# Product of probabilities and values with the values as weights, in a fused attention and two-layer kernel

## The chip, the cores and the metric

The kernel runs on one core of one Trainium2 chip. The metric is device time in microseconds (us), from the first to the last instruction and what lies around them; the median of several runs counts. All engines run their own instructions in program order and wait for each other by semaphores: TensorE (PE, its weight loads written PEld), VectorE (DVE), ScalarE (ACT), GpSimd (POOL), and SyncE (SP), which issues the DMAs.

## The reference

Eight batches of eight heads; 576 tokens, 64 features per head, 32 packed queries `p` per head. Two attentions come one after the other, the second reading the first one's result as keys and values, then two wide layers with an activation each.

```python
def sm_attn(qq, kk, vv):
    s = scale * np.matmul(qq, kk.transpose(0, 1, 3, 2))
    s = s - np.max(s, axis=-1, keepdims=True)
    a = np.exp(s)
    a = a / (np.sum(a, axis=-1, keepdims=True) + 1e-09)
    return np.matmul(a, vv)
p_packed = sm_attn(p, k, v)
out = sm_attn(q, p_packed, p_packed)
```

The result, as 4608 rows of 512, goes through `w_in` (512x2048), a leaky ReLU and `w_out` (2048x512), and then through a second pair of the same sizes with the activation h / (1 + exp(-1.702 h)).

## The kernel before, in words

The first part, up to about 310 us, makes both attentions and the first wide product; the rest (L694, L728, L847) is the other three wide products, which the change doesn't touch.

Per batch the first part has these steps, each a generator whose `yield`s cut it into pieces. `s1` makes the scores of the packed queries (L243), their maximum, and e = exp(scores) on ScalarE (L269). The four head pairs stand on the partitions, 32 packed queries each, so a tile of 128 partitions holds four heads; `par` is the even or odd head of each pair, so e is 128 x 2 x 576. Its last piece adds the sums and takes the reciprocal r (L273, L274). `packed` transposes e on PE in pieces of 128 keys (L284) and a rest of 64 (L286), copies the result to `et` (L289 on ScalarE, L291 on VectorE), and multiplies with the values v (L301): `et` is the stationary operand (32 packed queries of one head), v the moving one (64 features), and the result has queries on the partitions. L307 multiplies by r, L310 transposes to features on the partitions, and L313 copies that to `ppk`. From `ppk` come the second attention's scores (`s2`) and, folded with w1, the tiles `m` (`prod_m`) by which the wide product L369 (`l1`) works; L378 is its activation.

The order of all engines' work is written out. For batches 0 to 2 it is the list of words START: `score0` is the next piece of `s1(0)`, `pack0` of `packed(0)`, `l5` and `r5` a wide product and its activation, `w12` a piece of the conversion of w1 from float64 words (L155, L156, L159, L162, L163), `warm2` two products that only keep PE busy (L389). From then on there is one wide product per step n (six matmuls, about 0.8 us), and `side(n)` issues the pieces due behind it. Batch b+1, b from 2 to 6, has its pieces at s = 32 b plus

```python
first, second = range(-5, 1), (1, 2, 2, 4, 5, 6, 7)
third, fourth, fifth = (9, 10, 11, 12, 13, 14, 16, 17), (9, 10, 12, 13, 16, 20, 22, 23), (15, 23, 24, 24, 25)
for piece, when in ((s1(b + 1), first), (packed(b + 1), second), (s2(b + 1, 0), third),
```

so the sums stand at s and the transposes behind the product of s + 1. A piece called when a generator has ended does nothing. `aux` gives one of five PSUM banks in turn.

Of the kernel before, what the change touches and what calls it, by code (L numbers as in the profile page):

```python
# [9 lines left out]
F32 = mybir.dt.float32  # L10
# [4 lines left out]
ALU = mybir.AluOpType  # L15
# [3 lines left out]
B, H, S, D, J = 8, 8, 576, 64, 32  # L19
DM, FF = H * D, 2048  # L20
NT = B * S
P = 128
# [56 lines left out]
def packed_attention_moe_moe_kernel(tc, qT, kT, vm, vt, pT, w_in1, w_out1, w_in2, w_out2, out):  # L79
# [4 lines left out]
    nc = tc.nc  # L84
# [26 lines left out]
    with ExitStack() as ctx:  # L111
# [87 lines left out]
        px, pa = pools["px"], pools["pa"]  # L199
# [3 lines left out]
        ident = px.tile([P, P], F32, name="ident")  # L203
# [5 lines left out]
        tk, tq, tv, tp, e1, ppk, a2, mm = {}, {}, {}, {}, {}, {}, {}, {}  # L209

        def aux(name):
            return ps.tile([P, 512], F32, tag="aux", name=name, bufs=5)
# [21 lines left out]
        def after(load, b):  # L234
            if b < B:
                load(b)

        def both(tiles, lhsT, rhs, n):

            for i in range(4):  # L240
                for par in range(2):
                    r = slice(64 * par, 64 * par + 64)
                    nc.tensor.matmul(tiles[par][32 * i:32 * i + 32, :n], lhsT=lhsT(r, i, par), rhs=rhs(r, i),  # L243
                                     start=True, stop=True)

        def s1(b):
            k, p = tk.pop(b), tp.pop(b)
            t = [[None, None], [None, None]]
            for hf in range(2):
                for par in range(2):  # L250
                    t[par][hf] = aux(f"s1_{b}_{par}_{hf}")
                both([t[0][hf], t[1][hf]], lambda r, i, par: p[r, 2 * i + par, :],
                     lambda r, i: k[r, i // 2, i % 2, hf * TH:hf * TH + TH], TH)
            if b:
                after(load_k, b + 1)
                after(load_p, b + 1)
            yield
            mx, sm = (px.tile([P, 2, 2], F32, tag=w, name=f"{w}_{b}") for w in ("mx", "sm"))
            nb, r = (px.tile([P, 2], F32, tag=w, name=f"{w}_{b}", bufs=2) for w in ("nb", "r"))
            e = px.tile([P, 2, S], F32, tag="e", name=f"e_{b}")  # L260
            e1[b] = e, r
            for par in range(2):
                for hf in range(2):
                    nc.vector.reduce_max(mx[:, par, hf:hf + 1], t[par][hf][:, :TH], axis=AX.X)
                nc.vector.tensor_scalar(nb[:, par:par + 1], mx[:, par, 0:1], mx[:, par, 1:2], -SCALE, op0=ALU.max, op1=ALU.mult)
                yield
            for par in range(2):
                for hf in range(2):
                    nc.scalar.activation(e[:, par, hf * TH:hf * TH + TH], t[par][hf][:, :TH], AF.Exp, bias=nb[:, par:par + 1],  # L269
                                         scale=SCALE, accum_out=sm[:, par, hf:hf + 1])  # L270
                yield
            for par in range(2):
                nc.vector.tensor_scalar(r[:, par:par + 1], sm[:, par, 0:1], sm[:, par, 1:2], 1e-9, op0=ALU.add, op1=ALU.add)  # L273
            nc.vector.reciprocal(r, r)  # L274

        def packed(b):

            e, r = e1.pop(b)
            et = px.tile([P, 2, 5, P], F32, tag="et", name=f"et_{b}")
            t = [aux(f"t1_{b}_{par}") for par in range(2)]  # L280
            rest = aux(f"tr_{b}")
            for par in range(2):
                for k in range(4):
                    nc.tensor.transpose(t[par][:, P * k:P * k + P], e[:, par, P * k:P * k + P], ident)  # L284
            for par in range(2):
                nc.tensor.transpose(rest[:64, P * par:P * par + P], e[:, par, 512:576], ident)  # L286
            yield
            for par in range(2):
                nc.scalar.copy(et[:, par, 0:4, :], t[par].rearrange("p (k n) -> p k n", k=4))  # L289
            yield  # L290
            nc.vector.tensor_copy(et[:64, :, 4, :], rest[:64, :2 * P].rearrange("p (a n) -> p a n", a=2))  # L291
            yield
            v = tv.pop(b)
            o = px.tile([P, 2, D], F32, tag="o", name=f"o_{b}")
            t = aux(f"pp_{b}")
            for par in range(2):
                for k in range(5):
                    n = P if k < 4 else 64
                    for i in range(4):
                        c0 = D * (2 * (i % 2) + par)  # L300
                        nc.tensor.matmul(t[32 * i:32 * i + 32, D * par:D * par + D], lhsT=et[:n, par, k, 32 * i:32 * i + 32],  # L301
                                         rhs=v[:n, i // 2, k, c0:c0 + D], start=(k == 0), stop=(k == 4))
            if b:
                after(load_v, b + 1)
            yield
            for par in range(2):
                nc.vector.tensor_scalar(o[:, par, :], t[:, D * par:D * par + D], r[:, par:par + 1], None, op0=ALU.mult)  # L307
            yield
            t = aux(f"t2_{b}")
            nc.tensor.transpose(t[:, :P], o.rearrange("p a d -> p (a d)"), ident)  # L310
            yield
            ppk[b] = pw.tile([P, 4, J], F32, tag="ppk", name=f"ppk_{b}", bufs=2)
            nc.scalar.copy(ppk[b], t[:, :P].rearrange("p (i j) -> p i j", i=4))  # L313
# [98 lines left out]
        for b in range(2, B - 1):  # L412
            s = 32 * b
# [3 lines that stand above are left out]
                                (s2(b + 1, 1), fourth), (prod_m(b + 1, 0), fifth)):  # L417
                pieces(piece, [s + k for k in when])
# [146 lines left out]
        for b in range(3):  # L565
            going |= {f"score{b}": s1(b), f"pack{b}": packed(b)}
            going |= {f"attn{b}{hf}": s2(b, hf) for hf in range(2)}
            going |= {f"m{b}{c}": prod_m(b, c) for c in range(4 if b < 2 else 1)}
# [3 lines left out]
        for word in START:  # L572
# [4 lines left out]
            elif word[0] == "l":  # L577
                n = int(word[1:])
                banked[n] = l1(*order[n])
                side(n)  # L580
            elif word[0] == "r":
                n = int(word[1:])
# [97 lines left out]
        for k, (blk, p, f) in enumerate(steps):  # L680
# [10 lines left out]
            n = BLOCKS["b"][blk][1]  # L691
            for c in range(2):
                for m, (ws, xs) in enumerate(((0, 0), (0, 1), (1, 0))):
                    nc.tensor.matmul(acc[BANK[p]][:, c, :n], lhsT=w[:, ws, c], rhs=x[xs],  # L694
                                     start=(p in OPENS and f + m == 0), stop=(f == NJ - 1 and m == 2), skip_group_check=True)
# [65 lines left out]
        for m in range(1, 3 * NJ):  # L761
            n = first[m // NJ, m % NJ]
# [74 lines left out]
        for k, (blk, p, f) in enumerate(last_steps, LATER):  # L837
# [5 lines left out]
            n = BLOCKS["d"][blk][1]  # L843
# [63 lines left out]
```

## Time and profile before

| what | us |
|---|---|
| median of 3 runs | 1380.24 |
| lowest | 1379.56 |
| highest | 1765.2 |
| profiled execution | 1380.77 |
| its span, first to last instruction | 1378.6 |
| PE busy | 1354.9 (98%) |
| DVE busy | 1047.1 (76%) |
| ACT busy | 768.7 (56%) |
| mean granted clock of PE | 0.995 |

The profile is of one execution. A matmul in fp32 stands as two loads and two passes. Records of PE overlap: their lengths hold the way through the array, and what a pass costs is the distance from one start to the next. The form `128*32` beside a name is the part of the array that is used, rows by columns.

### The profile page before, as it was taken

The numbers are of one execution on the slowest core, as the hardware profiler recorded it, in microseconds if no ns is written. First come the engines' busy times: TensorE is split into PE (matmuls) and PEld (weight loads), VectorE is DVE, ScalarE is ACT, GpSimd is POOL, SyncE is SP. The second block draws the span as 40 slices with busy tenths as digits, with TensorE's granted clock in tenths as the row PEclk, the third lists the DMA queues.
The fourth block names the chain that finished last, engine by engine and source line by source line (L and its number), as shares of the span: only waits on it lengthen the run. The fifth ranks groups of instructions, "written<-read, shape, count | busy, mean of one in ns | idle before, by whom it ended". The sixth has DMA issues, their size and how long they took to land.

```text
span 1378.6 us, 23200 instructions
## 1 busy us (share of the span) xinstructions
PE 1354.9 (98%) x8746; PEld 1245.2 (90%) x8746; DVE 1047.1 (76%) x1548; ACT 768.7 (56%) x1363; POOL 98.5 (7%) x71
## 2 busy tenths in 40 slices
PE   6899999999999999999999999999999999999998
PEld 4688888889999989889999999999999899999998
DVE  6867777766989898989776657565559987878786
ACT  4756666676645545445566666666556443434342
POOL 2301111100000212100001000000000000000000
PEclk8999999999999999999999999999999999999999
DMA  9879999789646566564477777868886727263432
GB/s 335 303 238 311 315 318 319 255 289 328 210 165 205 174 204 225 165 235 144 137 259 237 257 244 251 266 212 261 267 289 208 222 65 215 72 189 98 139 102 46
DMA packets 251503, 302.46 MB, mean 219 GB/s; under 512 B 56832, under 2 KB 214528, under 8 KB 251392
## 3 DMA queue, kind: packets, MB, share of 16 engines
q1 hardware_dynamic: 248992, 300.70, 66.4%
q8 instruction: 68, 1.11, 0.3%
q10 hardware_dynamic: 2400, 0.30, 0.1%
q14 instruction: 43, 0.35, 0.1%
HBM read 184.55 MB, written 116.39 MB: 218 GB/s over the span
## 4 chain that ended last, share of the span: by engine, by line
PE 88%; DMA 4%; DVE 3%; ACT 3%; SPq 1%; issue 1%; POOL 0%; DVEq 0%; POOLq 0%; ACTq 0%
PE y L694 25%; PE h L728 24%; PE sum L847 18%; PE h L369 10%; PE first L847 7%; PE m L243 1%; DMA raw<-in_w_in_dram 1%; PE s L243 1%; DMA g_scratch<-g 1%; ACT g L378 1%; PE pp L301 1%; SPq L173 1%; ACT m L354 1%; DMA k<-in_kT_dram 1%; DMA q<-in_qT_dram 1%
## 5 line engine op out<-in xcount | busy, mean ns | idle before, releaser
L728 PE MATMUL h<-ya,wj 128*128 128x384 f32 x2016 | 349.9, 334 | 0.1
L728 PEld LDWEIGHTS h<-ya,wj 128*128 128x128 f32 x2016 | 349.4, 188 | 0.5 <-DVE g L750 0.4
L369 PEld LDWEIGHTS h<-a,m 128*128 128x128 f32 x1536 | 209.0, 190 | 33.8 <-issue 12.5
L500 ACT CAST da<-dr 128x960 fp32r<-128x960 f32 (+1 forms) x139 | 134.1, 966 | 179.1 <-PE sum L847 111.8
L369 PE MATMUL h<-a,m 128*128 128x288 f32 x1536 | 223.1, 301 | 8.8 <-ACT g L378 4.4
L694 PE MATMUL y<-ba,wo 128*128 128x480 f32 (+1 forms) x1080 | 225.9, 370 | 0.0
L694 PEld LDWEIGHTS y<-ba,wo 128*128 128x128 f32 x1080 | 205.4, 195 | 19.7 <-DVE ba L140 0.8
L500 ACT CAST ba<-br 128x960 fp32r<-128x960 f32 (+1 forms) x140 | 135.3, 966 | 150.5 <-PE y L694 130.7
L140 DVE TENSOR_TENSOR da<-dr,da 128x960 fp32r<-128x960 f32 (+1 forms) x139 | 154.1, 1111 | 44.1 <-ACT da L500 39.6
L140 DVE TENSOR_TENSOR ba<-br,ba 128x960 fp32r<-128x960 f32 (+1 forms) x140 | 164.9, 1180 | 19.5 <-ACT ba L500 17.6
L847 PE MATMUL sum<-da,wo 128*128 128x480 f32 (+1 forms) x840 | 176.0, 369 | 0.0
L847 PEld LDWEIGHTS sum<-da,wo 128*128 128x128 f32 x840 | 159.8, 193 | 14.8 <-DVE da L140 0.9
L378 ACT ACTIVATE g<-h 128x288 f32<-128x288 f32 x256 | 103.2, 422 | 79.9 <-PE h L369 62.7
L694 PE MATMUL y<-ba,wo_early 128*128 128x480 f32 (+1 forms) x600 | 125.7, 370 | 0.3 <-DVE ba L140 0.3
L694 PEld LDWEIGHTS y<-ba,wo_early 128*128 128x128 f32 x600 | 114.1, 195 | 11.0 <-DVE ba L140 0.7
L163 POOL TENSOR_TENSOR b_wo<-raw_wo 128x512 int32<-128x512 int32 x32 | 42.8, 1336 | 561.1 <-DVE raw_wo L162 308.3
L140 DVE TENSOR_TENSOR wj<-stage,wj 128x512 fp32r<-128x512 f32 x96 | 59.4, 619 | 26.3 <-ACT wj L667 25.8
L847 PE MATMUL sum<-da,wo_early 128*128 128x480 f32 (+1 forms) x360 | 75.4, 369 | 0.0
L847 PEld LDWEIGHTS sum<-da,wo_early 128*128 128x128 f32 x360 | 68.6, 193 | 6.0
L750 DVE TENSOR_TENSOR g<-v,h 128x384 f32<-128x384 f32 x48 | 26.5, 551 | 52.0 <-PE h L728 51.9
L357 DVE TENSOR_TENSOR m<-m,m 128x512 fp32r<-128x512 f32 x64 | 42.4, 685 | 29.6 <-ACT m L354 28.2
L734 ACT ACTIVATE g<-g 128x384 f32<-128x384 f32 x96 | 50.3, 524 | 18.7 <-ACT wj L667 6.2
(131 smaller groups left out, 1484.5 us busy)
## 6 DMA issues: line engine op xcount, KB each, us to landing
g_scratch<-g SPq DMA_DIRECT2D x64, 576.0 KB, 5.8
g_scratch<-g SPq DMA_DIRECT2D x96, 384.0 KB, 3.3
br<-g_scratch SPq DMA_DIRECT2D x64, 480.0 KB, 6.6
dr<-g_scratch SPq DMA_DIRECT2D x64, 480.0 KB, 4.7
stage<-wi_scratch SPq DMA_DIRECT2D x72, 256.0 KB, 4.0
wo_scratch<-b_wo SPq DMA_DIRECT2D x32, 448.0 KB, 4.8
k<-in_kT_dram SPq DMA_DIRECT2D x16, 576.0 KB, 7.5
q<-in_qT_dram SPq DMA_DIRECT2D x16, 576.0 KB, 6.4
```

Of the source, the lines that this page charges most:

```text
L140: at(step + 1, lambda: nc.vector.tensor_sub(*rest))
L163: nc.gpsimd.tensor_tensor(to.bitcast(I32), v.bitcast(I32), d, op=ALU.add)
L243: nc.tensor.matmul(tiles[par][32 * i:32 * i + 32, :n], lhsT=lhsT(r, i, par), rhs=rhs(r, i), start=True, stop=True)
L357: nc.vector.tensor_sub(m[:, 1, par, :], t[par], m[:, 0, par, :].bitcast(F32))
L369: nc.tensor.matmul(t[:, :TH], lhsT=m[:, ws, par, o:o + P], rhs=a[:, xs, par, :], start=(k == 0), stop=(k == 5))
L378: nc.scalar.activation(g1t[g][:, f % 2, hf * TH:hf * TH + TH], t[:, :TH], AF.Prelu, alpha=0.01)
L500: nc.scalar.copy(hi, src)
L694: nc.tensor.matmul(acc[BANK[p]][:, c, :n], lhsT=w[:, ws, c], rhs=x[xs], start=(p in OPENS and f + m == 0), stop=(f == NJ - 1 and m == 2), ...
L728: nc.tensor.matmul(to, lhsT=w[:, ws, COMBO[p], P * kk:P * kk + P], rhs=x[:, xs, kk, :], start=(p in UNIT_OPENS and kk + s == 0), stop=(kk ...
L734: nc.scalar.activation(to, to if src is None else src, AF.Gelu_apprx_sigmoid)
L750: nc.vector.tensor_add(g[1][:, HB:], v, d)
L847: nc.tensor.matmul(column_of(acc4[BANK[p]], c)[:, :n], lhsT=w[:, ws, c], rhs=x[xs], start=(p in OPENS and f + m == 0), stop=(f == NJ - 1 a ...
```

## The change

Two things are changed in `s1` and `packed`. The last piece of `s1` now takes the reciprocal of each sum by itself and multiplies e by it on VectorE, 576 elements on 128 partitions, once for each `par`; so the probabilities are divided by their sum ahead of the transposes. In `packed` the product has its operands swapped: 64 columns of v are the stationary operand and 32 packed queries of `et` the moving one, with 64 features on the partitions for each `par` and the heads along the free dimension. The loop over heads i is outermost, then keys k, then `par`. The result needs neither L307 nor L310, so two pieces of `packed` go, and the copy to `ppk` is its fifth piece instead of its seventh.

```diff
-            e1[b] = e, r
+            e1[b] = e
...
-            nc.vector.reciprocal(r, r)
+                nc.vector.reciprocal(r[:, par:par + 1], r[:, par:par + 1])
+                nc.vector.tensor_scalar(e[:, par], e[:, par], r[:, par:par + 1], None, op0=ALU.mult)
...
-            o = px.tile([P, 2, D], F32, tag="o", name=f"o_{b}")
             t = aux(f"pp_{b}")
-            for par in range(2):
+            for i in range(4):
                 for k in range(5):
                     n = P if k < 4 else 64
-                    for i in range(4):
+                    for par in range(2):
                         c0 = D * (2 * (i % 2) + par)
-                        nc.tensor.matmul(t[32 * i:32 * i + 32, D * par:D * par + D], lhsT=et[:n, par, k, 32 * i:32 * i + 32],
-                                         rhs=v[:n, i // 2, k, c0:c0 + D], start=(k == 0), stop=(k == 4))
+                        nc.tensor.matmul(t[D * par:D * par + D, 32 * i:32 * i + 32], lhsT=v[:n, i // 2, k, c0:c0 + D],
+                                         rhs=et[:n, par, k, 32 * i:32 * i + 32], start=(k == 0), stop=(k == 4))
             if b:
                 after(load_v, b + 1)
-            yield
-            for par in range(2):
-                nc.vector.tensor_scalar(o[:, par, :], t[:, D * par:D * par + D], r[:, par:par + 1], None, op0=ALU.mult)
-            yield
-            t = aux(f"t2_{b}")
-            nc.tensor.transpose(t[:, :P], o.rearrange("p a d -> p (a d)"), ident)
             yield
```

## Rows read from the trace of the kernel before

**Rows 1.** The page: busy times of PE, and the chain by line.

```profile
PE 1354.9 (98%) x8746; PEld 1245.2 (90%) x8746; DVE 1047.1 (76%) x1548; ACT 768.7 (56%) x1363; POOL 98.5 (7%) x71
...
PE y L694 25%; PE h L728 24%; PE sum L847 18%; PE h L369 10%; PE first L847 7%; PE m L243 1%; DMA raw<-in_w_in_dram 1%; PE s L243 1%; DMA g_scratch<-g 1%; ACT g L378 1%; PE pp L301 1%; SPq L173 1%; ACT m L354 1%; DMA k<-in_kT_dram 1%; DMA q<-in_qT_dram 1%
```

**Rows 2.** Waits of PE, 110 to 310 us: us in total, times, longest.

```profile
PE h L369 <- ACT g L378: 1.3, 3, 0.6
```

**Rows 3.** Waits of PE, 0 to 110 us.

```profile
PE t L310 <- DVE r L273: 1.6, 1, 1.6
...
PE t L310 <- DVE o L307: 0.8, 1, 0.8
```

**Rows 4.** Stretches of 10 us: engines' busy time, clock, DMA share, GB/s.

```profile
20.00:30.00 10.00, 8.89 (x112) 5.44 (x102) 8.41 (x17) 5.13 (x10) 3.49 (x3) 0.66 0.96 370
30.00:40.00 10.00, 6.99 (x57) 5.83 (x57) 9.72 (x21) 6.38 (x15) 1.26 (x1) 0.69 0.96 350
```

**Rows 5.** L301 alone, batch 2: length, passes, loads, clock, DMA, by stretch.

```profile
79.83:80.41 0.58, 0.58 (x32) 0.49 (x32) 1.00 0.29 80
80.41:80.66 0.25, 0.25 (x15) 0.15 (x8) 1.00 1.00 387
...
81.24:81.38 0.14, 0.14 (x15) 0.14 (x8) 1.00 1.26 428
```

**Rows 6.** L301 in its first section: ns shortest, median, longest.

```profile
L301 PEld LDWEIGHTS pp<-v,et x32: 106/110/111, 79.8 to 80.2; 128*32 128x32 f32 x32
L301 PE MATMUL pp<-v,et x32: 219/219/244, 79.8 to 80.3; 128*32 128x64 f32 x32
```

**Rows 7.** L389, 10.5 to 13.6 us: the same columns.

```profile
L389 PEld LDWEIGHTS keep<-ident x24: 186/192/192, 10.6 to 13.1; 128*128 128x128 f32 x24
L389 PE MATMUL keep<-ident x24: 274/275/377, 10.6 to 13.2; 128*128 128x128 f32 x24
```

**Rows 8.** Instructions on tile e: the same columns.

```profile
L284 PEld LDWEIGHTS t<-ident,e x64: 137/141/143, 13.8 to 262.7; 128*128 128x128 f32 x64
...
L286 PEld LDWEIGHTS tr<-ident,e x16: 110/111/113, 15.4 to 262.9; 128*64 128x64 f32 x16
```

**Rows 9.** Groups, 0 to 400 us: busy us, mean ns, idle before.

```profile
L329 DVE TENSOR_TENSOR wf<-wf,s2m 128x576 f32<-128x576 f32 x16 | 12.1, 758 | 0.6
...
L159 DVE TENSOR_SCALAR raw_wo<-raw_wo 128x512 uint32<-128x512 uint32 x16 | 6.8, 427 | 18.3 <-ACT raw_wo L156 14.7 <-DMA g_scratch<-g 3.2 <-DMA raw_wo<-in_w_out_dram 0.4
```

**Rows 10.** Timeline of batch 4: start, us, instruction, idle before.

```profile
153.91 0.21 DVE L273 TENSOR_SCALAR r<-sm 128x1 f32<-128x1 f32 x1
...
154.50 1.04 PE L284 MATMUL t<-ident,e 128*128 128x128 f32 x8
154.70 0.23 ACT L269 ACTIVATION_READ_ACCUMULATOR e<-s,nb 128x1 f32 x1
...
154.97 0.21 DVE L273 TENSOR_SCALAR r<-sm 128x1 f32<-128x1 f32 x1 [0.85 <-ACT e L269]
155.22 0.17 DVE L274 RECIPROCAL r<-r 128x2 f32<-128x2 f32 x1
```

**Rows 11.** Timeline of batch 3.

```profile
117.83 0.33 DVE L273 TENSOR_SCALAR r<-sm 128x1 f32<-128x1 f32 x2
```

**Rows 12.** Timeline of batch 2 at L310.

```profile
82.83 0.30 PE L310 MATMUL t<-ident,o 128*128 128x128 f32 x1
...
82.89 6.62 PE L369 MATMUL h<-a,m 128*128 128x288 f32 x48
```

**Rows 13.** Timeline around the last conversion of w1.

```profile
59.96 0.96 DVE L159 TENSOR_SCALAR raw<-raw 128x512 uint32<-128x512 uint32 x1
...
61.79 1.29 POOL L163 TENSOR_TENSOR w<-raw,w 128x512 int32<-128x512 int32 x1 [1.16 <-ACT m L354]
...
63.45 1.95 PE L243 MATMUL m<-w,ppk 64*32 64x512 f32 x32
```

**Rows 14.** Timeline of batch 0 behind L313.

```profile
23.46 1.21 PE L243 MATMUL s<-q,ppk 64*32 64x288 f32 x16 [0.35 <-ACT ppk L313]
```

More of the change, by code (lines that the diff above doesn't have):

```diff
@@ L273, in s1 @@
                 nc.vector.tensor_scalar(r[:, par:par + 1], sm[:, par, 0:1], sm[:, par, 1:2], 1e-9, op0=ALU.add, op1=ALU.add)
-            nc.vector.reciprocal(r, r)
+                nc.vector.reciprocal(r[:, par:par + 1], r[:, par:par + 1])
+                nc.vector.tensor_scalar(e[:, par], e[:, par], r[:, par:par + 1], None, op0=ALU.mult)
         def packed(b):
-            e, r = e1.pop(b)
+            e = e1.pop(b)
             et = px.tile([P, 2, 5, P], F32, tag="et", name=f"et_{b}")
```

## The prediction, written before the result

> **What bounds the kernel now.** I read the page's busy times and chain first [rows 1]. TensorE (PE) is busy for 98% of the span, the chain runs through its products line after line, and of the lines of the change only L301 is among the shown ones, with 1%. So the change has no large share to win, and what counts is where PE works without a gap and where it waits. The waits of PE by stretch answer that: from 110 to 310 us, where batches 3 to 7 are made, PE waits for others for 1.3 us in all [rows 2]; before 110 us it does wait, and two of those waits belong to the lines that go [rows 3]. So from about 60 us on every nanosecond that the change puts on PE is paid in full, while before that the start is a chain of loads, ScalarE and VectorE work (VectorE, DVE, is busy 8.4 and 9.7 of the 10 us from 20 and from 30 [rows 4]), into which PE fits. The eight batches split so: 0 and 1 in the start, 2 at its end, 3 to 7 under a saturated PE.
>
> **Products with values as weights.** Before, one batch's products are 40 fp32 matmuls, 80 loads and 80 passes in the trace, in four strips of the array 32 columns wide. The view by stretches shows one batch in four sections, long for the four full tiles of keys, short for the last 64 [rows 5]: 0.58 + 0.25 + 0.58 + 0.14 = 1.55 us. A long section is 8 rounds on each strip, a short one 2. So 6 rounds are 0.58 - 0.25 = 0.33 us, 0.055 us each. The first passes of a section last 244 ns where the median is 219 [rows 6]: 25 ns is the load of 32 columns, seen only once per section; the next loads hide under passes of 64 moving columns. What is left of a short section, 0.25 - 0.025 - 0.055 = 0.17 us, is the end of its passes and the change of tile shape (0.06 in the last, where the next work has the same shape).
>
> After, there are again 80 loads and 80 passes, but in two strips of 64 columns, so 16 rounds become 32 for the full tiles of keys and 4 become 8 for the rest; and the loop over heads outside makes eight sections instead of four. The pass has 32 moving columns, half of 55 ns, some 28. Its load is now the long one. For loads the trace has two ends: 32 columns 25 ns, and 128 columns 377 - 275 = 102 ns [rows 7]; the lengths of the load records agree (110 and 192 ns, 82 more for 96 columns) [rows 6, 7]. On that line 64 columns take 25 + 32 x 82/96 = 52 ns, which a pass of 28 cannot hide, so a round is about 55 ns. A section's remainder falls by half a pass to 0.14. Long: 0.052 + 7 x 0.055 + 0.14 = 0.58; short: 0.052 + 0.055 + 0.14 = 0.25; four of each, less 0.11 at the end, 3.2 us. That is 1.6 us more per batch. Against it speaks the only load of 64 columns in the trace, that of the transposes, whose record (111 ns) is no longer than one of 32 columns [rows 6, 8]; by it the load is 30 ns, a round 29, and the batch 2.2 us, 0.6 more. I take the first, because transposes load faster at 128 columns too (141 against 192 ns [rows 7, 8]) and so are another kind of load. The other end is a load and a pass that take turns, 80 ns a round: 4.0 us, 2.4 more. A gain is excluded: twice the rounds of half the length stream as long as before, and four more changes of shape come on top. Six batches (2 to 7) under a saturated PE: 6 x 1.6 = 9.8 us with the figure unrounded (1.64), between 3.8 and 14.6.
>
> The rule that bears on this price is in the Trainium skill, TensorE: Matmul & The Clock Gate, section "LDWEIGHTS (loading the stationary operand)": a load takes its columns divided by 1.2 GHz, whatever the rows. By it 64 columns are an estimated 53 ns and six batches cost 9.9 us; by the transposes' row they cost 3.8. The rows at 32 and 128 columns agree with the rule, the row at 64 does not, and no product of the kernel before loads 64.
>
> **Probabilities divided by their sum.** Before, the transposes of e wait for the exponentials alone. After, each half of e (the even or the odd heads) waits for sum, reciprocal and a 128x576 multiplication on DVE. For its price: a one-source DVE instruction of 512 fp32 words takes 427 ns, a two-source one of 576 takes 758 [rows 9]. 427 x 576/512, with some 150 ns fixed, is about 0.45 us; the upper end is 0.76. I take 0.45, as the new instruction has one source, in SBUF. The Trainium skill, VectorE: DVE Perf Modes, "Mode 2×_2P", gives such an instruction two elements per cycle for fp32 too; its rule and the 427 ns row go together, and by the 758 ns row the five waits below would cost 6.3 us in place of 4.5.
>
> Where it lies: batch 4's stretch (it repeats for 5, 6 and 7 at 190, 226 and 262 us) shows the transposes starting at 154.50, the first sum at 153.91, the second at 154.97, held by the last exponential's sum, which ends at 154.93 [rows 10]. New: second sum 154.97, + 0.21 + 0.03 + 0.17 (reciprocal) + 0.03 + 0.45 = 155.86, and 0.1 until PE sees it. The second half's transposes begin at about 155.95 instead of 154.94 (four at 0.109 after 154.50). PE has nothing else in its order, so 1.0 us is lost, four times. The first half, ready at 154.80, hides in it. In batch 3 both sums come at 117.83 [rows 11]; two chains back to back end at 119.5, the second half starts near 119.6 instead of 119.1: 0.5 us. Together 4.5 us. Queued behind on PE are the next products with w1, and through them ScalarE's activations; all just move with PE. DVE itself pays 0.9 us for two multiplications and 0.2 for one more reciprocal, less 0.4 for the two scalings that go, per batch; in these stretches it has gaps of 0.4 to 0.9 us around the sums [rows 10], so this costs nothing more.
>
> **What goes.** The scaling L307, off PE's path from batch 2 on. The transpose L310: the next product follows it after 0.06 us [rows 12]; six times is 0.3 us won. The copy L313 comes two steps earlier, which no one waits for from batch 3 on. The next values' load stays behind the products in SP's queue, 1.6 us later and tens of us ahead of its use.
>
> **The start.** Batch 1: PE waits 1.61 us for L310, from 58.14 to 59.75 [rows 3]. That goes, but its products end 1.6 us later, and they stand just ahead: nothing is won. Batch 2: the multiplications stand on DVE ahead of the last conversion of w1 (L159 at 59.96, with the GpSimd step of 61.79), and GpSimd holds them as it holds L159, which takes 0.96 us there instead of 0.43 [rows 9, 13]. That conversion lands some 1.2 us later; the product of w1 that needs it starts at 63.45, 0.4 us after its present end. I put 0.85 us. Batch 0: transposes wait until about 18 us instead of 15, partly unseen, as the copies of et stand behind work on w1 in ScalarE's order anyway. Products start 0.5 later and last longer, some of it at the lower clock (0.66 granted on the mean from 20 to 30 us, between 1.2 and 2.4 GHz [rows 4]); in return the copy L313 follows them at once, without the 0.75 us wait for L310 [rows 3]. From 23.46, the next step [rows 14], I expect 0 to 1.5 us later, and take 0.65. Together 1.5, between -1 and +3.
>
> **Sum.** 9.8 + 4.5 - 0.3 + 1.5 = 15.5 us. The profiled execution's 1380.77 us (span 1378.6 and 2.2 around it) becomes 1396.3; it stands 0.5 above the median of 1380.24, so I forecast 1395.7 us.
>
> **Rivals.**
> Narrow price for wide loads: each product batch is 0.6 dearer, not 1.6. For it the transposes' load, against it the line from 32 to 128 columns. 3.8 + 4.5 - 0.3 + 1.5 = 9.5: 1389.7 us.
> Load and pass in turn: a round of 80 ns, as two strips offer fewer places to load ahead. Against it: on four strips loads run ahead of passes now. 14.6 + 4.5 - 0.3 + 1.5 = 20.3: 1400.5 us.
> Not slower: the start decides. The chain through L307 and L310 is gone, and its PE waits of 1.6, 0.75 and 0.35 us (the last ahead of 23.46 [rows 14]) all move the rest up, 2.7 us. This wins only if the six products and five waits together cost less, under 0.25 us each, with loads hidden wholly. At no cost there, 1377.5 us. For it: those waits are real; against it: the eight sections and the 155.86 above.
>
> **How the numbers follow.** My forecast 0.62, cheap loads 0.20, loads in turn 0.13, not slower 0.05. The range goes from 1386 us (cheap loads and a start that wins 1 to 3 us) to 1402 (loads in turn, with a slower start or the slow multiplication). 2% is 27.6 us, about what a measurement of this kernel tells from no change. Even all upper ends, 14.6 + 6.3 - 0.3 + 3 = 23.6 us, stay within it: slower by over 2% needs something not seen here, such as a longer time at half clock, 0.04; faster by over 2%, 0.01; within it, 0.95.
>
> **What would show it.** Products of one batch at about 3.2 us with eight sections, their load records near 137 ns (110 + 27); transposes of batches 4 to 7 waiting for the DVE multiplication for about 1 us, in two pieces; multiplications of 0.45 us; no wait at L310's old place; from 310 us on the same durations as before. Wrong it would be if the load record is 111 ns, if the multiplication takes 0.76, or if the start moves by more than 3 us.

## The result and the profile after

The changed kernel takes 1398.63 us (median of 5 runs, 1397.25 to 1402.38), the kernel before 1379.56 beside it (the lowest of 5 runs is 1377.94). The ratio of the mean times is 1.0146, with a 95% interval from 1.0127 to 1.0166: slower by 1.5%; one run of the kernel before, far slower than its others at 1765.2 us, is left out of it. The profiled execution took 1400.15 us with a span of 1398.4, that is 19.8 us more than the span before.

The page of the changed kernel, busy times of PE and the chain by line, answers to [rows 1]:

```profile
PE 1372.3 (98%) x8738; PEld 1258.8 (90%) x8738; DVE 1056.4 (76%) x1556; ACT 769.8 (55%) x1363; POOL 98.4 (7%) x71
...
PE y L688 24%; PE h L722 20%; PE sum L841 18%; PE h L363 10%; PE first L841 7%; PE pp L301 2%; PE m L243 2%; PE s L243 1%; DMA g_scratch<-g 1%; DMA stage<-wi_scratch 1%; SPq L173 1%; ACT g L372 1%; DMA raw<-in_w_in_dram 1%; DMA raw_wo<-in_w
```

PE is still busy for 98%: it was given longer work, not more idle time alone. Eight instructions fewer stand on PE (the transposes L310), and yet its busy time grew by 17.4 us. The products L301 went from 1% to 2% of the chain.

**The products.** L301 alone by stretches, in batch 2 of the changed kernel (columns as in [rows 5]). The first four stretches are its first four sections, from one change of tile shape to the next:

```profile
80.72:81.27 0.55, 0.55 (x18) 0.51 (x18) 1.00 0.20 80
81.27:81.54 0.27, 0.27 (x8) 0.23 (x6) 1.00 0.93 358
81.54:82.10 0.56, 0.56 (x20) 0.52 (x18) 1.00 1.01 379
82.10:82.37 0.27, 0.27 (x8) 0.23 (x7) 1.00 0.94 350
80.72:83.87 3.15, 3.15 (x80) 2.86 (x80) 1.00 0.50 187
```

A long and a short section take 0.83 us and there are four pairs; before, there were two pairs, of 0.83 and 0.72 us. The pass and load records answer to [rows 6]:

```profile
L301 PEld LDWEIGHTS pp<-et,v x80: 129/138/138, 80.7 to 83.8; 128*64 128x64 f32 x64, 64*64 64x64 f32 x16
L301 PE MATMUL pp<-et,v x80: 219/223/243, 80.7 to 83.8; 128*64 128x32 f32 x64, 64*64 64x32 f32 x16
```

The load record is 138 ns, 28 more than at 32 columns. A pass of half the moving columns shows nearly the same length (223 ns against 219): its record holds the way through the array. The starts tell the price: within a section one round (a load and a pass on each of the two strips) follows the other after 58 ns.

**The waits.** PE's waits of the changed kernel from 110 to 335 us, the stretch of batches 3 to 7, for [rows 2], and the longest of those before 110 us, for [rows 3]:

```profile
PE t L285 <- DVE e L275: 2.0, 5, 0.4
PE t L285 <- ACT e L269: 1.5, 4, 0.4
PE h L363 <- ACT g L372: 1.3, 3, 0.6
...
PE t L285 <- DVE r L273: 4.8, 2, 3.9
```

The first two lines are new. The last is that of batches 0 and 1, whose transposes wait for 3.9 and 0.9 us behind VectorE; the two waits at L310 are gone. The second names ScalarE, but the timeline of batch 4, for [rows 10], shows that this engine is not what PE waits for:

```profile
158.76 0.21 DVE L273 TENSOR_SCALAR r<-sm 128x1 f32<-128x1 f32 x1
159.00 0.16 DVE L274 RECIPROCAL r<-r 128x1 f32<-128x1 f32 x1
...
159.20 0.52 DVE L275 TENSOR_SCALAR e<-e,r 128x576 f32<-128x576 f32 x1
159.55 0.23 ACT L269 ACTIVATION_READ_ACCUMULATOR e<-s,nb 128x1 f32 x1
...
159.82 0.21 DVE L273 TENSOR_SCALAR r<-sm 128x1 f32<-128x1 f32 x1
...
159.87 0.63 PE L285 MATMUL t<-ident,e 128*128 128x128 f32 x4 [0.36 <-ACT e L269]
160.06 0.16 DVE L274 RECIPROCAL r<-r 128x1 f32<-128x1 f32 x1
160.26 0.52 DVE L275 TENSOR_SCALAR e<-e,r 128x576 f32<-128x576 f32 x1
...
160.93 0.63 PE L285 MATMUL t<-ident,e 128*128 128x128 f32 x4 [0.43 <-DVE e L275]
161.28 0.22 PEld L287 LDWEIGHTS tr<-ident,e 128*64 128x64 f32 x2
161.39 0.38 PE L287 MATMUL tr<-ident,e 128*64 128x128 f32 x2
```

The first multiplication ends at 159.72 and PE starts 0.15 us later; the second ends at 160.78 and PE starts again 0.15 later. The exponential's last sum, at 159.55 + 0.23, belongs to the second half of e and merely came last in time: in each of batches 4 to 7 PE starts 0.15 us behind the end of the multiplication, in both halves, and only 0.07 to 0.10 us behind that sum. So PE stops twice per batch, in the two halves. The idle time of these lines, some 0.8 us per batch, is less than what a batch loses (1.17 us in the ledger below), since a record of PE holds the way through the array behind the last start.

**A fall of the clock.** Engines by stretch in the changed kernel, columns as in [rows 4], with POOL's busy time ahead of the clock: the last batch's product, and what stands behind it:

```profile
281.10:284.40 3.30, 3.30 (x86) 2.98 (x87) 1.12 (x2) 1.60 (x4) 0.68 (x1) 1.00 0.69 213
284.40:287.80 3.40, 3.40 (x34) 0.66 (x32) 0.00 (x0) 0.00 (x0) 0.60 (x1) 0.50 0.42 127
```

The kernel before from 110 to 310 us, where its batches 3 to 7 stand:

```profile
110.00:310.00 200.00, 197.37 (x2209) 168.16 (x2208) 139.35 (x323) 132.23 (x338) 21.23 (x16) 1.00 0.89 302
```

From 284.4 to 287.8 us the granted clock is 0.50, the 1.2 GHz level, where the kernel before has 1.00, the 2.4 GHz level, from 41 us on. PE had been busy throughout the product when it fell. The tiles m of that stretch come out 1.67 us late.

**The ledger.** The 256 activations of the first wide product (L378 before, L372 after) come in the same order in both kernels, the last of them at 325.6 us of the kernel before, where the first part really ends; so each pair's difference of starts in the timeline tells how far the work has been shifted. Where it grows:

| place | grows by, us | forecast |
|---|---|---|
| start, up to batch 2's product | 0.84 | 1.5 |
| products: batch 2 1.29, batches 3 to 7 1.95 each | 11.0 | 9.5 (L310's gain taken off) |
| transposes: batch 3 0.76, batches 4 to 7 1.17 each | 5.4 | 4.5 |
| clock 0.50 behind batch 7's product | 1.7 | 0 |
| rest up to 325 us | 0.1 | 0 |
| behind 325 us | 0.7 | 0 |
| sum (unrounded) | 19.8 | 15.5 |

### The profile page after: what moved, and what is told of

Its sections match the earlier page's. It is cut to its first block, busy times and chain, and to the rows that moved or that the text cites. A ratio compares the mean times of both kernels' runs of the same rounds, so it can differ in the third digit from the quotient of the medians.

```text
span 1398.4 us, 23190 instructions
## 1 busy us (share of the span) xinstructions
PE 1372.3 (98%) x8738; PEld 1258.8 (90%) x8738; DVE 1056.4 (76%) x1556; ACT 769.8 (55%) x1363; POOL 98.4 (7%) x71
## 3 DMA queue, kind: packets, MB, share of 16 engines
q8 instruction: 68, 1.11, 0.3%
## 4 chain that ended last, share of the span: by engine, by line
PE 85%; DMA 5%; DVE 4%; ACT 3%; SPq 2%; issue 1%; POOL 1%; POOLq 0%; DVEq 0%; ACTq 0%
PE y L688 24%; PE h L722 20%; PE sum L841 18%; PE h L363 10%; PE first L841 7%; PE pp L301 2%; PE m L243 2%; PE s L243 1%; DMA g_scratch<-g 1%; DMA stage<-wi_scratch 1%; SPq L173 1%; ACT g L372 1%; DMA raw<-in_w_in_dram 1%; DMA raw_wo<-in_w_out_dram 1%; POOL b_wo L163 1%
## 5 line engine op out<-in xcount | busy, mean ns | idle before, releaser
L372 ACT ACTIVATE g<-h 128x288 f32<-128x288 f32 x256 | 103.0, 419 | 98.6 <-PE h L363 81.4
L163 POOL TENSOR_TENSOR b_wo<-raw_wo 128x512 int32<-128x512 int32 x32 | 42.8, 1338 | 580.5 <-DVE raw_wo L162 364.5
L351 DVE TENSOR_TENSOR m<-m,m 128x512 fp32r<-128x512 f32 x64 | 42.4, 685 | 45.2 <-ACT m L348 43.7
L744 DVE TENSOR_TENSOR g<-v,h 128x384 f32<-128x384 f32 x48 | 26.5, 552 | 51.3 <-PE h L722 51.2
```

Source lines behind the costliest of these rows:

```text
L163: nc.gpsimd.tensor_tensor(to.bitcast(I32), v.bitcast(I32), d, op=ALU.add)
L351: nc.vector.tensor_sub(m[:, 1, par, :], t[par], m[:, 0, par, :].bitcast(F32))
L372: nc.scalar.activation(g1t[g][:, f % 2, hf * TH:hf * TH + TH], t[:, :TH], AF.Prelu, alpha=0.01)
```

## The experiments

The shifts in the experiments are read by the same pairs of activations, their products from the first to the last start.

**The division alone.** The operands of the product, L307 (as a copy without the factor) and L310 stay as in the kernel before.

```diff
-            nc.vector.reciprocal(r, r)
+                nc.vector.reciprocal(r[:, par:par + 1], r[:, par:par + 1])
+                nc.vector.tensor_scalar(e[:, par], e[:, par], r[:, par:par + 1], None, op0=ALU.mult)
...
-                nc.vector.tensor_scalar(o[:, par, :], t[:, D * par:D * par + D], r[:, par:par + 1], None, op0=ALU.mult)
+                nc.vector.tensor_copy(o[:, par, :], t[:, D * par:D * par + D])
```

> The kernel before with the division alone moved ahead of the transposes; the product keeps its old operands, its result is copied without a factor and still transposed. Theory of two parts: the transposes of batches 4 to 7 wait about 1.1 us each for the second multiplication and those of batch 3 about 0.7, as in the changed kernel, and the products keep 1.55 us; about +5.3 us from there and up to +1 from the start, some 1385 to 1386 us. Rival, that the wait comes only with the new product (its later end pushing the rest): the transposes wait for less than 0.3 us and the time stays within 1 us of 1379.6.

Measured: 1386.95 us against 1378.42, ratio 1.0064, 1.0049 to 1.0079, one microsecond above the time expected. PE's waits from 110 to 335 us in this kernel:

```profile
PE t L285 <- DVE e L275: 2.0, 5, 0.4
PE t L285 <- ACT e L269: 1.4, 4, 0.4
```

They are those of the changed kernel, and the shift grows by 0.75 in batch 3 and by 1.18 in each of batches 4 to 7: 5.5 us, with products of 1.51 us as before. The start is 0.66 later. So the waits are the division's, in place and size.

**The swap alone.** The changed kernel without the multiplication L275: the probabilities are not divided by their sum at all.

```diff
-                nc.vector.reciprocal(r[:, par:par + 1], r[:, par:par + 1])
-                nc.vector.tensor_scalar(e[:, par], e[:, par], r[:, par:par + 1], None, op0=ALU.mult)
+            nc.vector.reciprocal(r, r)
```

> The changed kernel without the multiplication of e, so the division is left out; sums and reciprocals stay. Theory of two parts: each batch's product still takes 3.3 us from its first pass to the next work, the transposes of batches 3 to 7 start without a wait, and about 5.3 us of the 19 go: 1392 to 1394 us. A drop of the granted clock behind a product, as in batch 7 of the changed kernel (1.7 us), may or may not come. Rival, that the waits of the transposes are covered elsewhere: 1397 to 1399 us.

Measured: 1395.53 us (1392.18 to 1398.54), ratio 1.0124, 1.0102 to 1.0145, between the time expected and the rival's. The one wait of PE left from 110 to 335 us in this kernel:

```profile
PE h L362 <- ACT g L371: 1.2, 3, 0.5
```

The records of its product's loads in batch 2:

```profile
L300 PEld LDWEIGHTS pp<-et,v x80: 128/138/139, 80.8 to 84.0; 128*64 128x64 f32 x64, 64*64 64x64 f32 x16
```

The transposes no longer wait; products of 3.14 us add 1.29 in batch 2 and 1.95 in each of 3 to 7, just as in the changed kernel. A fall of the clock stands behind batch 7's product here too (279.2 to 282.6 us) and costs the same 1.66. The first part is 13.7 us late, and 2.3 more come behind 325 us. The two halves' first parts, 6.5 and 13.7 us, add up to 20.2; the changed kernel has 19.1. Most of the difference lies in the starts, 0.66 and 1.0 us late here and 0.84 there.

**Narrower weights.** The 64 columns in two pieces of 32: four strips of the array, twice the loads and passes.

```diff
-                    for par in range(2):
-                        c0 = D * (2 * (i % 2) + par)
-                        nc.tensor.matmul(t[D * par:D * par + D, 32 * i:32 * i + 32], lhsT=v[:n, i // 2, k, c0:c0 + D],
+                    for c in range(0, 2 * D, 32):
+                        par, c0 = c // D, D * 2 * (i % 2) + c
+                        nc.tensor.matmul(t[c:c + 32, 32 * i:32 * i + 32], lhsT=v[:n, i // 2, k, c0:c0 + 32],
```

> The changed kernel with each product of 64 columns of v cut into two of 32, on four strips instead of two: twice as many loads and passes, each load 32 columns, moving columns as changed. If the load of 64 columns sets the round (load records of 138 ns in place of 110, rounds of 58 ns), rounds fall to about 30 ns, a product to about 2.2 us in place of 3.3, and the time by 6 to 8 us to 1391 to 1393. Rival, a least time per round on a strip whatever the load: rounds stay 58 ns and the product 3.3 us, time 1398 to 1399. Rival, a cost for each instruction: 160 in place of 80 make it 4 us or more, 1402 or more.

Measured: 1407.70 us, ratio 1.0215, 1.020 to 1.023: slower, not faster. Yet in batches 1, 2, 6 and 7 the product took 2.21 us as expected. The records of its loads in batch 2:

```profile
L301 PEld LDWEIGHTS pp<-et,v x160: 102/113/114, 81.0 to 83.2; 128*32 128x32 f32 x128, 64*32 64x32 f32 x32
```

PE's timeline of its batch 3:

```profile
124.34 1.57 PE L301 MATMUL pp<-et,v 128*32 128x32 f32 x105
127.60 1.01 PE L301 MATMUL pp<-et,v 128*32 128x32 f32 x51 [1.68 <-issue]
```

What its instruction queue moved from 124 to 128 us (packets, MB, share):

```profile
q8 instruction: 1, 0.02, 1.5%
```

And PE's waits from 110 to 335 us at this line:

```profile
PE pp L301 <- issue: 6.5, 3, 3.0
```

In batches 3 to 5 PE stands still in the middle of the product ("issue": it waits for nothing that the profile shows), for up to 3.0 us. Each time a packet of the instruction queue is in flight for part of it. That PE had run out of instructions fits this, with 160 loads and passes in about 2 us, but it wasn't tried by itself. Behind each of the three standstills the clock falls to 0.50, for 3.4, 3.4 and 6.8 us. So the undisturbed products, with rounds of 32 ns, confirm the price of a load, and the standstills with their falls of the clock cost more than the shorter loads won. They also rule out the two rivals named above, a least time per round and a cost for each instruction. The width of a load and the number of strips changed together in this run; no run parts the two.

**Later transposes, product later too.** All five pieces of `packed`, the product and the copy of its result too, stand one step later.

```diff
-            first, second = range(-5, 1), (1, 2, 2, 4, 5, 6, 7)
+            first, second = range(-5, 1), (2, 3, 3, 5, 6, 6, 7)
```

> The changed kernel with the transposes of batches 3 to 7 one step (one wide product, 0.8 us) later, and the copies, the product and the copy of its result one step later too. Theory: the second multiplication ends 1.1 us after the place where the transposes stood, so one step takes 0.8 us of the wait of 1.1 and what is left is 0.3 or less; 4 to 5 us less than the changed kernel, 1393.5 to 1395. Rival, that the wait only moves to the copies and the product: no gain, 1397 to 1399.

Measured: 1400.96 us (1399.31 to 1403.26), ratio 1.0167, 1.0152 to 1.0182; not faster. PE's waits for the division from 110 to 335 us:

```profile
PE t L285 <- DVE e L275: 0.7, 4, 0.2
```

Engines by stretch in the same kernel, two products and what stands behind each of them:

```profile
127.50:131.10 3.60, 3.60 (x83) 3.14 (x82) 0.99 (x2) 0.89 (x2) 1.29 (x1) 0.99 0.78 267
131.10:134.50 3.40, 3.40 (x15) 3.40 (x16) 0.74 (x2) 1.83 (x6) 0.00 (x0) 0.50 0.69 207
243.70:247.10 3.40, 3.40 (x83) 3.00 (x81) 0.94 (x2) 0.89 (x2) 1.29 (x1) 1.00 1.05 374
247.10:250.50 3.40, 3.40 (x16) 3.40 (x15) 0.50 (x1) 1.59 (x5) 0.00 (x0) 0.50 0.56 186
```

The wait did shrink, from 3.5 us to 0.7, and the undisturbed batches 4, 5 and 7 cost 2.5 us instead of 3.1. At 325 us this profile is 2.6 us ahead of the changed kernel's. But the clock fell twice, for some 0.85 us each, and behind 325 us it lost 3.0 us where the changed kernel lost 0.7. The first part follows the theory, the median does not. The two longest of the four executions have a mean granted clock of 0.989 and 0.990, the other two 0.994 and 0.995.

**Sections joined.** Odd heads begin with the rest of 64 keys, so that short sections meet twice and long ones once: five stretches of one shape instead of eight.

```diff
-                for k in range(5):
+                order = (0, 1, 2, 3, 4) if i % 2 == 0 else (4, 0, 1, 2, 3)
+                for k in order:
...
-                                         rhs=et[:n, par, k, 32 * i:32 * i + 32], start=(k == 0), stop=(k == 4))
+                                         rhs=et[:n, par, k, 32 * i:32 * i + 32], start=(k == order[0]), stop=(k == order[-1]))
```

> The changed kernel with the keys' order turned round for every second head pair (the rest of 64 first), so that neighbouring sections share the array's shape: five stretches of one shape instead of eight, loads and passes the same. If each change of shape costs its drain and an unhidden load (about 0.15 us, of the 0.14 + 0.052 in the sum), a product falls from 3.3 to about 2.8 us and the time by 2.5 to 3.5 us, to about 1395.5. Rival, that the loads alone make the price: the product stays at 3.2 to 3.3 us and the time within 1 us of the changed kernel.

Measured: 1397.98 us, ratio 1.0144, 1.0122 to 1.0167. The product takes 2.78 us and adds 1.59 per batch instead of 1.95; three changes of shape less save 0.36 us, so one costs 0.12. The clock stays at 2.4 GHz behind all products. The start, however, is 3.9 us later than in the kernel before, against 0.84 in the changed one, and that takes back what was won.

**The kernel before with its sections joined** in the same way (the even heads of each pair begin with the rest of keys).

> The kernel before with the same idea alone: the even heads' rest of 64 keys first, the odd heads' last, so three stretches of one shape instead of four. If a change of shape costs about 0.15 us, each product falls from 1.55 to about 1.4 us, seven of them 1 us: 1378 to 1379 us. Rival: no difference, since the shapes' ends are hidden.

Measured: 1378.49 us against 1379.63, ratio 0.9995, 0.9984 to 1.0005: the same. The product is 1.38 us instead of 1.51, one change of shape less, and the profile gains 0.13 per batch in batches 3 to 7, as expected; a microsecond in all is too little for this measurement. The start of this profile is 2.2 us earlier than in the kernel before, which the edit does not explain (see "The start" below).

**All three.** Narrow weights, joined sections and later transposes together.

> The changed kernel with three mends: loads of 32 columns on four strips, sections joined so that the last has the shape of the next work, and the transposes one step later. If the three terms are what the change cost, the product is 1.8 to 1.9 us against 1.5 before, the waits for the multiplication are under 0.3 us, and the time comes back to within 3 us of the kernel before: 1378 to 1383. Rival, a cost of the change that none of the three holds: 1386 us or more.

Measured: 1399.21 us, ratio 1.0145, 1.0132 to 1.0159: nothing of the gain arrived, and the time is the rival's. The start is 5.5 us late. Products of 1.91 us in batches 1 to 3, but 2.37 to 4.23 in 4 to 7, where PE stands still again, by its waits from 110 to 335 us:

```profile
PE pp L302 <- issue: 4.7, 4, 2.1
```

**Later transposes, product in its place.** This parts what the fourth run had mixed: the product keeps its place beside the tiles m.

```diff
-            first, second = range(-5, 1), (1, 2, 2, 4, 5, 6, 7)
+            first, second = range(-5, 1), (2, 3, 3, 4, 5, 6, 7)
```

> The changed kernel with the pieces of packed at 2, 3, 3, 4, 5, 6, 7 steps in place of 1, 2, 2, 4, 5, 6, 7: the transposes stand one wide product later, the products with the values and all behind them stay where they were, next to the tiles m of the same shape. The run with the pieces at 2, 3, 3, 5, 6, 6, 7 brought the transposes' wait from 1.14 down to 0.30 us per batch, but parted product and m and had two drops of the clock. My theory: with the neighbours left together the wait alone goes, 4 x 0.84 + 0.4 = 3.8 us, so 1394.8 us, 1393.5 to 1396; a drop of the clock more or less than in the changed kernel (one, of 1.65 us) moves it by that much. Products stay at 3.14 us. Rival A: the product now stands one step behind the copies to et and waits for them, 0.4 us or more per batch: 1397 us, and the waits at L301 show it. Rival B: the time does not follow the wait at all, since what PE saves comes back as drops of the clock: 1398 to 1401 us.

Measured: 1403.33 us (1399.72 to 1406.55), ratio 1.0179, 1.0155 to 1.0203. PE's timeline of batch 5 from its transposes on:

```profile
202.63 0.63 PE L285 MATMUL t<-ident,e 128*128 128x128 f32 x4 [0.19 <-DVE e L275]
...
205.24 0.30 PE L301 MATMUL pp<-et,v 128*64 128x32 f32 x2 [0.18 <-ACT et L290]
205.73 3.36 PE L301 MATMUL pp<-et,v 128*64 128x32 f32 x78 [0.19 <-ACT et L290]
```

My theory fell and rival A's mechanism holds, though not its time: the wait only moves. Of the 1.17 us at the transposes 0.38 are left, but the product now waits for ScalarE's two copies to `et`, once for each half, and takes 3.63 us from first to last start. A batch costs 3.06 us instead of 3.12. The clock fell twice, in batches 3 and 4, and at 325 us this profile is 0.8 us behind the changed kernel's. The median is 4.7 above, more than the profiled execution explains, whose span is 1.1 longer. The two longer executions, 1405.42 and 1406.55 us, have a mean granted clock of 0.988, the profiled one 0.993; so more time at the low level goes with them, as rival B had it, but no trace of them was kept.

**That, and joined sections** in batches 2 to 7 alone.

> The same, and for batches 2 to 7 alone the order of keys is reversed for odd heads, so that short sections meet (eight changes of shape become five); batches 0 and 1 keep their order, as with all batches reversed the start had come out 3 us later. My theory: products of 2.78 us in batches 2 to 7 and 3.14 in 0 and 1, six times 0.35 = 2.1 us less than with the later transposes alone: 1392.7 us, 1391 to 1394.5, a start within 1 us of the changed kernel's. That is still some 13 us above the kernel before: the loads of 64 columns (6 x 1.3 us), the change of shape left over and the start stay. Rival: the later start of the run with joined sections came from elsewhere than the order in batches 0 and 1, or another drop of the clock takes the gain: 1395 to 1398 us.

Measured: 1399.12 us (1395.55 to 1400.35), ratio 1.0143, 1.0123 to 1.0163. A batch costs 2.69 us: the joined sections save 0.37 as expected, the later transposes next to nothing, as in the run before. And the start is 3.9 us late again, although batches 0 and 1 keep their order: my expectation of 1 us failed, and the order in batches 0 and 1 is not needed for it. In this profile as in that of the fifth run, the clock stands at 0.50 from 16.1 to 29.8 us, in that of the changed kernel from 18.2 to 21.6; batch 0's product is 5.19 and 4.76 us long, against 3.44. That this makes the start late is likely and not shown: with the swap alone batch 0's product took 5.57 us and the start was 1.0 late. The clock falls once more in batch 5.

## Why the prediction was right, and where it was off

The forecast was 1395.7 us, the measurement 1398.6, inside the range and on the side that was forecast. Against the profiled execution, by which the sum was made, 1396.3 stands beside 1400.15.

- **Loads of 64 columns set the products' round.** Right: forecast was a record near 137 ns, a round of 55 ns and 3.2 us a batch; the trace has 138, 58 and 3.14 from the first to the last start (3.29 with the step to the next work). The record of the transposes (111 ns for 64 columns) was the wrong witness: the cheap-loads rival, 2.2 us, is out, and so is the load and pass in turn, whose round would be 80. The run with 32-column pieces and its 2.21 us for twice as many matmuls says the same from the other side. The Trainium skill, TensorE: Matmul & The Clock Gate, section "LDWEIGHTS (loading the stationary operand)", puts a load at its columns over 1.2 GHz, an estimated 53 ns for 64; the trace agrees but for the 5 ns by which the round is longer.
- **The products' term was still too small, 9.5 against 11.0.** Of the 1.95 us in batches 3 to 7, 1.63 are the product's own length, as forecast (1.64). The rest is behind it. Before, the last short section, 32 columns wide, ran together with the tiles m of the same shape (the 0.06 us of the fourth section in [rows 5]); with 64 columns it no longer does, and the first wide product behind m comes 0.16 us later for it. L310's end gives back 0.10, a little more than forecast. But 0.27 are lost right behind its old place, and there the prediction had a step wrong: it put the earlier copy to `ppk` at nothing, since no one waits for it, but other work stands behind it. ScalarE's timeline of batch 7, first the kernel before, then the changed one with a wait of PE's loads:

```profile
270.37 0.58 ACT L354 CAST m<-m 128x512 fp32r<-128x512 f32 x1
...
272.41 0.30 ACT L313 COPY ppk<-t 128x128 f32<-128x128 f32 x1
```

```profile
289.33 0.26 ACT L307 COPY ppk<-pp 128x128 f32<-128x128 f32 x1
289.48 0.60 ACT L348 CAST m<-m 128x512 fp32r<-128x512 f32 x1
...
290.86 0.43 PEld L363 LDWEIGHTS h<-a,m 128*128 128x128 f32 x3 [0.25 <-DVE m L351]
```

  The copy now stands ahead of the first conversion of m, which starts 1.55 us behind the first wide product (287.93) instead of 1.41 (268.96), and the next tile m comes late for PE. No run moved that copy back, so its part is read from the timeline and not tried. In batch 2 of the kernel before PE's first pass for m stood 0.35 us ahead of the second, a gap that the changed kernel doesn't have; there the cost is 1.29.
- **The division.** Right in mechanism and place: 1.17 us in each of batches 4 to 7 against 1.0, and 0.76 in batch 3 against 0.5. The multiplication was mis-sized, 0.52 us where I had taken 0.45; the rows of the changed kernel, grouped up to 400 us (busy us, mean ns; the mean of L275 holds three of the start that ran beside GpSimd's L163 and took 0.66 to 1.39 us, the median is 521 ns):

```profile
L275 DVE TENSOR_SCALAR e<-e,r 128x576 f32<-128x576 f32 x16 | 10.2, 636 | 0.6
...
L273 DVE TENSOR_SCALAR r<-sm 128x1 f32<-128x1 f32 x16 | 3.3, 204 | 0.4
L274 DVE RECIPROCAL r<-r 128x1 f32<-128x1 f32 x16 | 2.6, 164 | 0.6
```

  The sum, on one element with its scalars read from a tile, takes 204 ns and the reciprocal, without such scalars, 164: I had put 150 ns as fixed. And PE starts 0.15 us behind the multiplication, not 0.1. Together the second half starts 1.11 us behind its sum (159.82 to 160.93) where 0.98 was forecast. The first half stops PE too, for 0.36 us, which I had not seen; but by the timeline this hides as forecast, since the second half's chain ends no earlier without it.
- **L310's end.** Right in that PE no longer waits at its place, before 110 us or behind it; what came in its place is said above.
- **The start.** 0.84 against 1.5, within -1 to +3, and its two terms came out unlike each other. Batch 2's was right: the last conversion of w1 on GpSimd starts 1.20 us later (62.99), and the wide product behind the tiles m 0.83 later (66.16), for 0.85; the release that PE's loads wait for there is that of VectorE's m (L351), which the multiplications push back by 1.21. Batch 0's 0.65 came to nothing: its next step starts at 25.13, 1.67 us later, but by 30.2 us PE is where it was. That is in part luck, for the clock was low from 18.2 to 21.6 us there, and before from 20.2 to 27.0. In the profiles of all eleven kernels the start goes with the time that the clock stands at 0.50 in the first 60 us: with 6.8 us (the kernel before with joined sections) it is 2.2 us earlier than in the kernel before, which has 13.7; with 10.2 to 13.7 it is 0.5 to 1.2 later (the changed kernel has 10.2), and with 20.5, in four kernels, 1.0 to 5.5 later. So 0.84 is one execution's figure. Where the low stretches fall, and why, stays open.
- **The clock** was named only as a way to be wrong. It fell to 0.50 behind batch 7's product, and cost 1.67 us.
- **Behind 325 us** I expected nothing, and the changed kernel lost 0.7 us there. By the starts of the wide products the shift shrinks by up to 1.0 us at 570 to 625 us of the kernel before, and grows at 675 to 725 and at 960 to 1035, by 0 to 1.5 us each in most kernels. Where it grows in the changed kernel, PE waits for VectorE's and ScalarE's activation steps g and h (L744, L740), 1.1 us in sum; the waits of PE in the kernel before show none there. Why is not explained; runs of the changed kernel alone differ by 5 us, and the longest has a mean granted clock of 0.991 where the others have 0.995 or 0.996.

The rival "not slower" needed under 0.25 us for each product and wait; they cost 1.95 and 1.17. No version with both the division and the swapped product came near the kernel before: the best three, at ratios of 1.0143 to 1.0145, stand level with the changed kernel.

## What to carry to other kernels

Before you swap the operands of a small product, count loads times stationary columns: in this kernel the load was the round once the moving side was shorter than the weights are wide, and halving the moving columns while doubling the weights' doubled the time. Normalising ahead of a transpose puts VectorE's sum, reciprocal and multiplication between the exponential and TensorE; moving the consumer later only helps as far as the next consumer has room, as the copies showed. And on a saturated engine the neighbours of an operation belong to its price: what shares its shape, what it had been hiding, and what stands behind its copies in another engine's order.

## What was not expected of the hardware

- **PE stands still amid many short instructions.** With 160 loads and passes in about 2 us, PE stood still for up to 3.0 us in mid-product (three times in one kernel, four in another from 110 to 335 us) with nothing that it waited for in the profile. With 80 in 3.1 us the waits of PE show none at the product, and a packet of the instruction queue in flight is not enough for it: one was, at 243.24 us, in batch 6's product of the changed kernel.
- **The clock fell behind wide-weight products.** In the six kernels with 64-column weights, batches 2 to 7, 7 of 36 products had a stretch at 0.50 begin in them or within 0.3 us of their end; in the three kernels with the 32-column weights of before, 0 of 18. One such stretch of 3.4 us cost 1.67 us where it fell on the tiles m, and some 0.85 where it fell on wide products. Seven are few: spread by chance over all 54 products, all seven would fall among the 36 about once in 21 times. The mean granted clocks of all executions point the same way, 0.990 to 0.995 on the average of each of the six kernels and 0.996 to 0.997 in the three, though they hold the start too. Why it hits one batch and not the next is open.
- **A change of tile shape costs 0.12 us**, by the run with joined sections (0.36 us for three; 0.14 for one in the kernel before), and the passes of m ran into the product's last ones where the shape was the same, and not where it differed.
